# Two more chunks of an mLSTM + FFN kernel attended in 64x64 quarters, and two FFN stages exchanged

## The chip, the cores and the metric

The kernel runs on one core of a Trainium2 chip. The core has a tensor engine (PE in the profile; its weight loads are listed as PEld), a vector engine (DVE), a scalar engine (ACT), GpSimd (POOL) and a sync engine (SP), whose only work here is to issue DMA transfers (its queue is SPq in the profile). Each engine carries out its own instructions in the order in which the program puts them. The metric is the device time of one execution in microseconds (us). All values are 32-bit floats.

## What is computed

An mLSTM cell feeds a feed-forward network with a squared ReLU:

```python
# mLSTM cell: q, k, v, o_gate of shape (4, 8, 768, 40); i_gate, f_gate of shape (4, 8, 768)
for t in range(S):
    m_new = max(f[t] + m, i[t])
    f_stab, i_stab = exp(f[t] + m - m_new), exp(i[t] - m_new)
    m = m_new
    C = f_stab * C + i_stab * outer(v[t], k[t])       # 40 x 40 for each of 4 x 8 heads
    n = f_stab * n + i_stab * k[t]
    y[t] = sigmoid(o[t]) * (C @ q[t]) / max(abs(n @ q[t]), 1)
# FFN on x = y as (3072, 320)
h = maximum(x @ w_in, 0)                              # w_in 320 x 2048
out = (h * h) @ w_out                                 # w_out 2048 x 320
```

## The kernel before

**Chunks.** The 768 steps of each batch are cut into 6 chunks of 128 steps, so there are 24 chunks, numbered `s` = 0 to 23. Within a chunk the cell is an attention: scores of keys and queries, multiplied by a matrix of decays `W`, times the values; across chunks it hands on the state `C`. Two chunks make one group of 256 tokens for the FFN; FFN1 is the product with `w_in`, FFN2 the one with `w_out`. Groups 0 and 1 take FFN1 in full; groups from 2 on take it by a recursive scheme of fewer block products (`ffn1_open`, `ffn1_rows`, `ffn1_close`), and FFN2 of groups from 1 on likewise (`ffn2_fast`).

**Old and new way of attending.** Chunks 0 to 5 (`X_SQ = 6`) go through `attend`: matmuls `hi` (queries times old state, L622), `dC` (state update, L634) and `hp` (weighted scores times values, L645), then `normalise`, which leaves rows of `x` in SBUF; `turn_rows` transposes these rows on the tensor engine (L848, L850) and ACT copies them to `xT` (L853). Chunks from 6 on go through `attend_begin` and `attend_end`: the same products in quarters of 64x64, which the array works on side by side (L708 for the state, L727 for the values, L738 for the update). Between begin and end stands a one-element DVE instruction (L700), on which the second half of the matmuls waits. Their result is transposed: `store_num` writes it to DRAM (L773), `load_num` reads it back in four transfers (L778), `normalise_turned` divides it and multiplies with the gate on DVE (L787 to L803), `store_rows` and `load_rows` send `x` through DRAM once more (L828, four of L833), and `turn_squares` ends the transposition on DVE (L840). `scale_q` (L672) multiplies the queries by their decays on DVE; the products of L708 read its result. `decays` (L488) makes those decays on ACT.

**Masks.** `mask` (L469) sets the entries of late keys in `A` to -1e30 on POOL, and then `weigh` takes exponentials on ACT (L511), eight instructions for a chunk.

**Order of the work.** The order is written out by hand and kept on every engine. After a prologue, a loop over `u` = 0 to 7 takes chunks 2 to 5, two values of `u` a chunk, with a quarter of FFN1 of group 0 (`u` < 4) or 1 in each (L874, L885). In an odd `u` it calls `attend`, transfers for later chunks (`load`, `pair_up`, `load_o`) and `transposes` of the next chunk (L549); in an even one `scores` (L583), `weighted` (L597) and `weigh`. All along it rounds the weights to a shorter format, one piece after another: `words` on ACT (L220, L222), `join` on DVE (L231, L235, L236) and POOL (L240), and the fetch of a later piece (L210), which waits for the buffer that `join` has freed. The sums of weights for the recursive scheme (`sums_of_win`: L1020, L1022, L1024, L1026) stand on DVE between these. A second loop over `n` takes the rest in parts, four to a chunk, from chunk 6 on: FFN1 of group 2 with chunk 6, FFN2 of group 0 with chunk 7 (L911), and then FFN2 of group g with an even and FFN1 of group g + 2 with an odd chunk.

In the odd passes `u` = 5 and 7 the transfers that SP is given after `attend` are, in this order:

```python
for r in {5: (8,), 7: (9,)}.get(u, ()):
    load(r)                      # 7 transfers
for r in {5: (7,), 7: (8,)}.get(u, ()):
    pair_up(r)                   # 4 transfers
if u > 4:
    load_o(2 * s)
    load_o(2 * s + 1)
```

## Time and profile before

| | us |
|---|---|
| median of three runs (lowest, highest) | 491.84 (490.12, 493.88) |
| the profiled execution: its time | 491.22 |
| its span from first to last instruction | 489.4 |

Where each engine is busy in the stages that the change touches (busy us in each stretch of the span):

| stretch, us | what PE does | PE | DVE | ACT | POOL |
|---|---|---|---|---|---|
| 40 to 60 | FFN1 of group 0, chunk 3 | 18.51 | 16.70 | 15.69 | 9.97 |
| 60 to 76 | chunk 4, FFN1 of group 1 | 15.44 | 10.25 | 13.79 | 4.58 |
| 76 to 91 | chunk 5, FFN1 of group 1 | 15.00 | 12.56 | 12.16 | 6.38 |
| 91 to 110 | chunk 6, FFN1 of group 2 | 19.00 | 15.46 | 12.62 | 6.78 |
| 110 to 131 | chunk 7, FFN2 of group 0 | 20.72 | 18.39 | 11.28 | 10.01 |
| 131 to 167 | chunks 8 and 9 | 36.00 | 24.22 | 13.55 | 23.78 |

The granted clock of the tensor engine is 1.00 in each of these stretches. A row of a timeline reads: start in us from the beginning of the span, duration in us, engine, line of the kernel, operation, result<-operands, how many were merged ("x8"), and in brackets the idle time before it with what ended that. A row of the chain of waits has the same first two columns and names the work that the end of the program hangs on at that time. Rows for one kind of instruction can be told apart by their line. One f32 matmul counts as two PE instructions.

### The profile page before, as it was taken

To read this page: it belongs to the slowest core of one execution; us is meant where nothing else is said; L and a number is where in the kernel's file an instruction comes from. 1 tells how busy PE (TensorE), PEld (TensorE's weight loads), DVE (VectorE), ACT (ScalarE), POOL (GpSimd) and SP (SyncE) were. 2 spreads that over 40 slices of the span, in tenths; PEclk is the share of its full clock that TensorE was granted. 3 is DMA by queue.
4 is the path that set the end of the run, shared out by engine and by line. 5 is a ranking of instruction groups with operands and counts; after the bars stand their busy time and mean duration, and the time that the engine had idled before them with its cause. 6 is when DMAs were issued, how large, how long until landed. Compare 5 with 4: busy or idle time off the path is not lost.

```text
span 489.4 us, 15237 instructions
## 1 busy us (share of the span) xinstructions
PE 481.7 (98%) x6169; PEld 449.0 (92%) x6169; DVE 341.8 (70%) x704; ACT 240.4 (49%) x531; POOL 215.3 (44%) x322
## 2 busy tenths in 40 slices
PE   9999999999999999999999999999999999999997
PEld 4886788897799999999999999999999999999996
DVE  7799767888946856957966956857856956635441
ACT  4676996764522650942742941742942640513300
POOL 6455533432679178078179078078174040020000
PEclk9999999999999999999999999999999999999999
DMA  9999997745878579758759778658665612200000
GB/s 185 227 243 227 304 230 183 151 84 140 171 130 199 120 138 225 134 107 212 135 99 219 140 117 208 134 109 213 123 106 129 149 51 82 55 28 2 3 27 29
DMA packets 191096, 68.08 MB, mean 139 GB/s; under 512 B 158833, under 2 KB 180241, under 8 KB 191025
## 3 DMA queue, kind: packets, MB, share of 16 engines
q1 hardware_dynamic: 185280, 57.50, 55.1%
q0 software_dynamic: 5600, 9.50, 8.1%
q8 instruction: 49, 0.80, 0.7%
q14 instruction: 23, 0.18, 0.1%
q10 hardware_dynamic: 144, 0.10, 0.1%
HBM read 54.77 MB, written 18.01 MB: 149 GB/s over the span
## 4 chain that ended last, share of the span: by engine, by line
PE 87%; ACT 5%; SPq 4%; DMA 3%; issue 1%; DVE 0%; ACTq 0%
PE h_ps L965 35%; PE h_ps L1041 26%; PE h_ps L1090 8%; PE h_ps L911 4%; PE h_ps L874 3%; PE numT L727 3%; PE numT L708 2%; DMA lent_t<-in_moe_w_in_dram 1%; PE numT L738 1%; SPq L210 1%; PE tp L575 1%; PE h_ps L575 1%; SPq L1151 1%; ACT g_c L511 1%; DMA raw<-in_moe_w_in_dram 1%; DMA og<-in_o_gate_dram 1%
## 5 line engine op out<-in xcount | busy, mean ns | idle before, releaser
L475 POOL TENSOR_SCALAR_AFFINE_SELECT A_bc<-A_bc 64x512 f32<-64x512 f32 x32 | 22.5, 704 | 80.4 <-ACT kq L492 57.9
L965 PE MATMUL h_ps<-T,S 128*128 128x160 f32 x352 | 51.7, 300 | 0.6 <-ACT g_c L1107 0.6
L1071 ACT COPY r_sb<-h_ps 128x512 f32<-128x512 f32 x18 | 10.5, 585 | 84.2 <-PE h_ps L1041 84.2
L965 PEld LDWEIGHTS h_ps<-T,S 128*128 128x128 f32 x352 | 48.9, 190 | 1.1 <-ACT g_c L1107 0.9
L965 PE MATMUL h_ps<-w_out,g 128*128 128x160 f32 x336 | 49.2, 303 | 0.0
L981 DVE TENSOR_TENSOR y_sb<-y_sb,h_ps 128x160 f32<-128x160 f32 x44 | 14.1, 320 | 47.7 <-PE h_ps L965 47.6
L965 PEld LDWEIGHTS h_ps<-w_out,g 128*128 128x128 f32 x336 | 46.1, 190 | 1.3 <-issue 0.5
L1041 PE MATMUL h_ps<-xT,w_in 128*128 128x128 f32 x320 | 42.8, 278 | 0.0
L1041 PE MATMUL h_ps<-lent_t,w_in 128*128 128x128 f32 x320 | 42.2, 275 | 0.0
L1041 PEld LDWEIGHTS h_ps<-xT,w_in 128*128 128x128 f32 x320 | 38.9, 192 | 1.4 <-issue 1.0
L1090 PE MATMUL h_ps<-xT,w_in 64*64 64x128 f32 x960 | 39.1, 272 | 0.0
L1041 PEld LDWEIGHTS h_ps<-lent_t,w_in 128*128 128x128 f32 x320 | 38.9, 192 | 0.2 <-issue 0.2
L1041 PE MATMUL h_ps<-lent_t 128*128 128x128 f32 x320 | 39.0, 275 | 0.0
L1041 PEld LDWEIGHTS h_ps<-lent_t 128*128 128x128 f32 x320 | 37.3, 192 | 0.0
L505 ACT ACTIVATE A_bc<-A_bc,b_R 128x64 f32<-128x64 f32 (+1 forms) x128 | 35.7, 361 | 1.8 <-POOL A_bc L475 1.4
L1090 PEld LDWEIGHTS h_ps<-xT,w_in 64*64 64x64 f32 x960 | 34.8, 133 | 1.3
L379 POOL DMA_DIRECT2D va<-in_v_dram x56 | 34.2, 619 | 1.8 <-DMA kq_rows<-in_q_dram 1.3
L758 DVE STREAM_TRANSPOSE tn<-numT 128x256 f32<-128x256 f32 x36 | 14.0, 428 | 28.5 <-PE numT L708 19.2
L874 PE MATMUL h_ps<-xT,w_in 128*128 128x256 f32 x128 | 30.1, 385 | 1.6 <-ACT xT L853 1.2
L874 PEld LDWEIGHTS h_ps<-xT,w_in 128*128 128x128 f32 x128 | 23.4, 190 | 6.1 <-POOL w_in L240 1.6
L1033 POOL TENSOR_TENSOR lent_t<-xT 128x128 f32<-128x128 f32 (+1 forms) x18 | 14.6, 833 | 32.7 <-DVE xT L840 32.7
L965 PE MATMUL h_ps<-w_out,g_c 128*128 128x160 f32 x192 | 28.0, 302 | 0.0
(218 smaller groups left out, 1150.0 us busy)
## 6 DMA issues: line engine op xcount, KB each, us to landing
A_bc<-a_slots SPq DMA_DIRECT2D x32, 256.0 KB, 4.4
num_rows<-tn SPq DMA_DIRECT2D x18, 256.0 KB, 2.3
kq<-num_rows SPq DMA_DIRECT2D x72, 64.0 KB, 2.1
raw<-in_moe_w_out_dram SPq DMA_DIRECT2D x7, 640.0 KB, 5.4
kqT<-kq_rows SPq DMA_DIRECT2D x34, 128.0 KB, 3.3
og<-in_o_gate_dram SPq DMA_DIRECT2D x24, 160.0 KB, 4.9
out_dram<-y_sb SPq DMA_DIRECT2D x24, 160.0 KB, 3.1
raw<-in_moe_w_in_dram SPq DMA_DIRECT2D x7, 512.0 KB, 6.9
```

The source lines that it names most:

```text
L379: eng.dma_start(dst[HALVES[n], PR * (1 - late_keys) : PR * (2 - late_keys)], src[HALVES[late_keys], PR * m : PR * (m + 1)],)
L475: nc.gpsimd.affine_select(part, part, compare_op=ALU.is_ge, fill=-1e30, base=0, pattern=[[0, PR], [0, 2], [1, DP]], channel_multiplier=-1,)
L505: nc.scalar.activation(A[0][:, x, to], A[0][:, x, to], AF.Exp, bias=b_R[:, b, c, own, x : x + 1],)
L727: nc.tensor.matmul(d["numT"][m][HALVES[e], i, t0:], lhsT=va_w[s % NKQ][keys, at * D1 : at * D1 + DP], rhs=rhs, start=(s % NB == 0 and i == ...
L758: nc.vector.transpose(to[:, 2 * m : 2 * m + 2], d["numT"][m].rearrange("p c t -> p (c t)"))
L874: nc.tensor.matmul(hs[i][:, n, :], lhsT=w_in[:, a, fb * P : (fb + 1) * P], rhs=xT[:, :, a, :], start=(n == 0 and a == 0), stop=False,)
L911: nc.tensor.matmul(o_ps, lhsT=st["g2", g][:, fb, j * P : (j + 1) * P], rhs=w_out[:, fb, :], start=(fb == 0), stop=(fb == NF - 1),)
L965: nc.tensor.matmul(to, lhsT=lhsT[:, p], rhs=rhs[:, p, :], start=(start and p == 0), stop=(p == NPAIR - 1), skip_group_check=True,)
L981: add = lambda to, a, b: nc.vector.tensor_tensor(to, a, b, op=ALU.add)
L1033: sub = lambda to, a, b: eng.tensor_tensor(to, a, b, op=ALU.subtract)
L1041: nc.tensor.matmul(to[:, n, :], lhsT=lhsT[:, 4 * q + n, :], rhs=rhs, start=(start and n == 0), stop=True, skip_group_check=True,)
L1090: nc.tensor.matmul(to[cols, n, :], lhsT=w_in2[rows, 4 * q + n, cols], rhs=rhs, start=(start and n == 0), stop=True, skip_group_check=True,)
```

## The change

- `X_SQ` goes from 6 to 4: chunks 4 and 5 are attended by `attend_begin` and `attend_end`, stored by `store_num`, read back by `load_num`, normalised by `normalise_turned`, and their `x` goes through DRAM (`store_rows`, `load_rows`, `turn_squares`) and not through `turn_rows`. The state of chunk 3 is read in its old layout, that of chunk 4 is kept in the new one in the same buffers (`C_flat`).
- The masks of chunks 4 and 5 are no longer put on `A` ahead of the exponentials, but on `W` behind them (`mask_W`, one POOL instruction). `weigh(4)` and the new `decays(4)` move on ACT ahead of the rounding step that they followed.
- In the loop over `n`, FFN2 of group 0 comes first, with chunk 6, and FFN1 of group 2 second, with chunk 7. `ffn1_begin` goes; FFN2 of group 0 holds two PSUM banks at a time. The sums for the recursive scheme move with them.
- A constant mask (`bdm`) goes; one product with it becomes two copies.

The core of the diff:

```diff
-    KQ_SQ, X_SQ, ROT = 7, 6, 8
+    KQ_SQ, X_SQ, ROT = 7, 4, 8
...
+    def mask_W(s):
+        nc.gpsimd.affine_select(
+            st[s]["W"], st[s]["W"], compare_op=ALU.is_ge, fill=0.0, base=0, pattern=[[0, H], [1, P]],
+            channel_multiplier=-1,
+        )
...
     for u in range(8):
...
-                turn_rows(s - 1)
+                if s - 1 < X_SQ:
+                    turn_rows(s - 1)
                 scores(s)
                 ffn1(u // 4, u % 4)
             if u == 2:
+                weigh(4, masked=True, vw=False)
+                decays(4)
                 rounding.words()
             weighted(s)
...
             if u == 2:
-                mask(s + 1)
                 rounding.join()
+                mask_W(4)
                 rounding.join()
-                weigh(s + 1, masked=True)
+                values(4)
                 rounding.words()
             else:
...
-                weigh(s + 1, masked=(u == 0), vw=(u > 0))
+                if u == 6:
+                    normalise_turned(4)
+                    store_rows(4)
+                weigh(s + 1, masked=(u != 6), vw=(u == 6))
+                if u == 4:
+                    mask_W(5)
                 square_half()
+                if u > 0:
+                    scale_q(s)
...
-            attend(s)
+            if s < X_SQ:
+                attend(s)
+            else:
+                attend_begin(s)
+                attend_end(s)
...
-            normalise(s)
+            if s < X_SQ:
+                normalise(s)
+            else:
+                store_num(s)
...
             if u > 4:
                 load_o(2 * s)
                 load_o(2 * s + 1)
+            if u == 7:
+                load_rows(4)
+                load_squares(7)
+            if u > 4:
+                load_num(s)
             transposes(s + 1, (True, True))
             rounding.words()
             ffn1(u // 4, u % 4)
             square_half()
+            if u == 5:
+                decays(5)
...
-    turn_rows(5)
-    load_squares(7)
+    turn_squares(4)
...
-    parts = [(1, 2, i) for i in range(4)] + [(2, 0, i) for i in range(4)]
-    for g in range(1, NG):
+    parts = []
+    for g in range(NG):
         parts += [(2, g, i) for i in range(4)]
         if g + 2 < NG:
             parts += [(1, g + 2, i) for i in range(4)]
...
+        if n == 0:
+            turn_kq(7)
+            normalise_turned(5)
+            store_rows(5)
+        if n == 1:
+            load_rows(5)
```

On each engine the new order is the program's own. On DVE it is, from chunk 4 on: `weighted(4)`, `scale_q(4)`, a `join`, L700 of chunk 4, its two transposes, its state, a `join`, a sum of weights, `weighted(5)`, `normalise_turned(4)`, `scale_q(5)`, a `join`, a sum of weights, L700 of chunk 5, its transposes, two `join`s, a sum of weights, `turn_squares(4)`, `weighted(6)`, `turn_kq(7)`, `normalise_turned(5)`, a `join`, L700 of chunk 6. On SP `store_num(4)` comes right behind the fetch of the `join` that follows chunk 4's state, then `load(8)`, `pair_up(7)`, two `load_o`, and `load_num(4)` behind these; one chunk later a fetch and `store_num(5)`, `load(9)`, `pair_up(8)`, two `load_o`, `load_rows(4)`, `load_squares(7)` and `load_num(5)`.

## The prediction, made before the changed kernel ran

> **What bounds the kernel now.** I read the page's busy times first, then the chain of waits from 56 to 142 us, then the timelines of PE, ACT, DVE and SP over that stretch. The busy line says that the tensor engine has no room:
>
> ```profile
> PE 481.7 (98%) x6169; PEld 449.0 (92%) x6169; DVE 341.8 (70%) x704; ACT 240.4 (49%) x531; POOL 215.3 (44%) x322
> ```
>
> The chain tells where that holds. From 49 to 60.5 us it runs over ACT; from 60.56 us to the end it is PE with hardly a gap. So behind 60.56 us an instruction taken from PE is worth its whole length, and anything that PE has to wait for costs its whole length. The rows for the parts that change, the old attend of chunk 4, the transposition of its x, and the new attend (of chunk 7, from its first matmul to its last):
>
> ```profile
> 65.35 1.05 PE hi L622 x8
> 66.40 0.89 PE dC L634 x8
> 67.29 1.75 PE hp L645 x16
> ...
> 74.47 0.37 PE tp L848 x2
> 74.83 0.37 PE tp L850 x4
> ...
> 114.54 0.38 PE numT L708 x8
> ...
> 115.64 0.17 DVE kq L700
> ...
> 116.75 0.22 PE numT L708 x8
> ```
>
> Two idle times stand in the stretch before, in the timelines of ACT and PE: ACT waits 4.27 us for a piece of the weights, and PE then waits 1.16 us for ACT.
>
> ```profile
> 48.93 0.68 ACT L220 ACTIVATE mag<-raw 128x512 f32<-128x512 f32 x1 [4.27 <-DMA raw<-in_moe_w_in_dram]
> ...
> 60.56 0.70 PE L874 MATMUL h_ps<-xT,w_in 128*128 128x256 f32 x2 [1.16 <-ACT xT L853]
> ```
>
> The last view is the one that decides. It is SP's timeline behind chunk 4, with no gap in it from 70.04 to 78.80 us:
>
> ```profile
> 70.04 0.37 SPq L210 DMA_DIRECT2D raw<-in_moe_w_out_dram  x1
> 70.51 0.42 SPq L367 DMA_DIRECT2D kq<-in_k_dram  x1
> 71.02 1.28 SPq L369 DMA_DIRECT2D kq<-in_k_dram  x2
> 72.40 2.57 SPq L379 DMA_DIRECT2D va<-in_v_dram  x4
> 75.02 1.25 SPq L347 DMA_DIRECT2D kq_rows<-in_k_dram  x2
> 76.31 1.23 SPq L347 DMA_DIRECT2D kq_rows<-in_q_dram  x2
> 77.59 1.21 SPq L417 DMA_DIRECT2D og<-in_o_gate_dram  x2
> ```
>
> That is 0.64 us for each of 13 transfers. In the kernel before nobody is waiting for them.
>
> **What the change takes off PE.** The attend of chunk 4 goes from 3.70 us (65.35 to 69.05) to the 2.43 us of chunk 7 (114.54 to 116.97, its wait for L700 included): -1.27. That of chunk 5, the last of its batch, has no update; it goes from 2.80 (81.01 to 83.81) to two passes each of L708 and L727, 0.38 + 0.44 + 0.22 + 0.46 = 1.50: -1.30. The two `turn_rows` go, 0.73 (74.47 to 75.20) and 0.74: -1.47. Chunk 7's scores come as in later chunks, 0.69 for 0.88: -0.19. FFN1 of group 2 and FFN2 of group 0 keep their matmuls, so that exchange is worth nothing by itself.
>
> **What it moves on ACT.** `weigh(4)` (2.43 + 0.20 us, now at 50.08) and two new decays (0.61 each, chunk 6's row) are 3.85 us; they go into the idle 4.27, so ACT is some 2.6 us earlier behind it. PE gets its 1.16 back and 0.24 by which an FFN1 quarter was stretched (3.86 for 3.62): -1.4, with 0 as the other end, should the next piece of weights then be late (it is issued at 45.28 and lands a median of 5.4 us later, at 50.7, so I take the -1.4). The POOL masks are of like size in another place, 1.28 and 1.09 us, and the decays of chunk 5 (1.22) meet 1.55 us of ACT idle at 74.49: no cost; without that cover they would delay a ReLU by 1.2. The constant mask and one product against two copies are under 0.5 us on POOL and DVE in the prologue, where the chain runs over DMA and ACT: taken as 0.
>
> All this makes -5.6 us, if no wait is added.
>
> **The first added wait: chunk 5's scaled queries.** Chunk 4's result now has to be back from DRAM before DVE gets to `scale_q(5)`, because `normalise_turned(4)` stands in front of it in DVE's order. Count from PE. Chunk 4 starts at 65.35 - 1.4 and ends 2.43 later, at 66.4. DVE then transposes (0.78), updates the state (0.35) and does a `join` (1.88, from 68.10 to 69.98): 69.4. Only then can SP's fetch start, which the `join` releases. SP needs the 8.76 us of the rows above, and 0.34 and a gap for `store_num`: 78.6. Four reads of `load_num` take 1.73 us to issue and the last lands 2.1 later (its median): 82.1. `normalise_turned` is 1.84 (107.70 to 109.54), `scale_q` 0.65: 84.6. PE comes to chunk 5 at 66.4 + 0.90 (L549) + 4.53 (FFN1 quarter) + 1.09 (scores) + 4.71 (next quarter) = 77.6. It waits +7.0 us.
>
> **The second: L700 of chunk 5.** PE does its first half in 0.82, to 85.4. DVE has a `join` and a sum of weights (1.88 + 1.21) between `scale_q(5)` and L700 (0.17), so it is there at 88.0 at best: +2.6. Chunk 5 ends at 88.7.
>
> **The third: weights of chunk 6.** PE goes on for 0.90 + 4.52 + 1.09 + 4.50 (a quarter of FFN2), to 99.7. DVE has `turn_squares(4)` ahead of `weighted(6)`, and that waits for `load_rows(4)`. Chunk 5's transposes and a `join` end at 88.7 + 0.78 + 1.88 = 91.4; then SP has the fetch and 13 transfers, 9.66 us in its second series (84.45 to 94.11), and 0.45 for the store: 101.5. Four of L833 take 1.86 at the least and land 2.2 after the last: 105.1. DVE turns (0.53) and weighs the first half (0.64): 106.3. PE waits +6.6, and 0.2 more for the second half.
>
> **The fourth: L700 of chunk 6.** In front of it DVE has `turn_kq(7)`, `normalise_turned(5)` and a `join`. `load_squares(7)` takes 3.1 us to issue (mean of four rows) and lands 3.4 after its last: 109.1; `load_num(5)` lands at 109.9 by then. So 109.1 + 1.23 + 1.84 + 1.88 + 0.17 = 114.2. PE, at 107.2 with its first half and 0.69 of scores in between, waits +6.3.
>
> Chunk 6 then ends at 114.9, with scores, chunk and a quarter of FFN2 done; the same work ended at 91.06 + 4.50 + 1.48 + 0.88 = 97.9 before. Items: -5.6 + 7.0 + 2.6 + 6.8 + 6.3 = +17.1.
>
> Next in line are the sums over x for FFN1 of group 2. DVE has them about 126.3 (`load_num(6)` landed 121.9, then 1.84, 1.45 and 1.06), PE asks at 114.9 + 13.12 = 128.0: covered, by under 2 us, and that much could be lost too. From chunk 8 on the order on PE is the old one, and PE is the bound again.
>
> Against the profiled execution, 491.22 (0.6 under the median of the three runs, which is nothing here): 491.2 + 17.0 = 508.2. PE also starts slowly after idling. The kernel's first matmuls, in the timeline, run at 424 ns each (12 in 5.09 us), later ones of the same form at 220:
>
> ```profile
> 0.94 5.30 PE L1140 MATMUL idle<-zeros 128*128 128x512 bf16 x12 [0.94 <-DVE zeros L1135]
> 7.27 1.03 PE L1140 MATMUL idle<-zeros 128*128 128x512 bf16 x4
> ```
>
> No gap in this trace is longer than 1.2 us, and none of those shows it, so I bound it: nothing, or 12 x 0.204 = 2.45 us for each of three gaps over 6 us, 7.4 in all. Only the last gap is followed by work that PE bounds, so I take half of one, +1: 509.
>
> By the Trainium skill ("TensorE: Matmul & The Clock Gate", Part 1) the array falls to half its clock after an idle window of about 3.4 us and needs as long a busy one to recover. An estimate by that page is 1.7 us lost for each gap, 5.1 for three, which would make the sum 513; it speaks against a change that opens such gaps, and the trace before has none long enough to test it.
>
> **The rivals.** (a) Forecast: all four waits, chance 0.65. SP's spacing is its bound: at the 0.43 us that a lone `load_num` read takes in the trace, each 13 transfers would be 2.7 us shorter, 5.4 off: 503; all of the slow clock: 516. (b) Only the first two: the 7 us in which PE stands still let SP catch up, and the third and fourth are covered: 491.2 - 5.6 + 9.6 = 495. It needs a fetch, 14 transfers and three more sets of four between 91.4 and about 99 us, 0.3 us each; the rows say 0.64. Chance 0.12. (c) On the other side, faster: the reads of chunk 4 are there in time, PE stays without gaps, and the -5.6 are all: 485.6. It decides at 75.1 us, when the data must have landed for DVE to have `scale_q(5)` done at 77.6; that is 7 us earlier than my count. For it speaks that in later chunks store and read back take under 6 us (store at 101.67, reads issued from 103.71 to 106.02); against it, that there nothing is queued between them. Chance 0.08. (d) Worse than the forecast, from slow clock and transfers that land later than their medians together (x rows take up to 6.2 us): 516 and more. Chance 0.15.
>
> **How the numbers follow.** The time is that of (a), 509. The range takes in (a) with its bounds (503 to 516), nearly all of (b) and the lower part of (d): 494 to 517. One per cent, about what a measurement can tell, is 4.9 us: faster than 486.9 is (c), 0.08; within is most of (b), 0.11; slower is the rest, 0.81.
>
> **What would show it.** PE's idle time in front of chunk 5's first L708, put down to DVE, of about 7 us; behind it one of 2 to 3 us in front of the second half; DVE idle at the normalisation's first instruction (L790 now) for `num_rows`, and at L840 for `x_rows`; SP without a gap for 8 us between the store and its reads. The 1.16 us in front of the first quarter of group 1 should be gone, and each attend shorter by 1.3. If SP issues these 13 transfers in 2 us, or the reads stand ahead of them, I am wrong, and (c) holds.

## The result and the profile after

| | before | after |
|---|---|---|
| median, us (lowest, highest, runs) | 491.36 (490.12, 493.88, 4) | 523.37 (522.60, 524.29, 4) |
| ratio, 95% interval | | 1.0645 (1.0597 to 1.0694) |
| profiled execution: its time, its span | 491.22, 489.4 | 524.09, 522.4 |

The change makes the kernel 32 us slower. The forecast was slower too, but 509 us with a range to 517, so it is 14 us short and outside its range. In the tables, times are medians of all runs; the ratios leave out one run each of e2 and e15, which fell in a slower state of the chip. First the page of the changed kernel: the busy times, the granted clock in 40 slices, and the chain that ended last by engine.

```profile
PE 487.0 (93%) x6229; PEld 452.7 (87%) x6229; DVE 341.5 (65%) x719; ACT 242.5 (46%) x534; POOL 218.4 (42%) x321
...
PEclk9999996868889999999999999999999999999999
...
PE 76%; SPq 8%; DMA 7%; DVE 4%; ACT 3%; issue 2%; POOL 0%; DVEq 0%; ACTq 0%; POOLq 0%
```

PE stands still for 35.4 us of the span (522.4 - 487.0) where it was 7.7 before. It is also busy 5.3 us longer, although the quarters are meant to take less of its time; the clock row dips in slices 7 to 12 (78 to 157 us). The chain now runs 15% over SP's queue and transfers (7% before). PE's timeline, its rows behind an idle time of over 1 us from 78 to 165 us:

```profile
88.12 0.70 PE L727 MATMUL numT<-kq,Co 40*64 40x128 f32 x8 [8.53 <-DVE kq L687]
91.23 0.70 PE L727 MATMUL numT<-kq,Co 40*64 40x128 f32 x8 [1.55 <-DVE Co L718]
...
110.17 1.30 PE L746 MATMUL numT<-A_bc,va 64*64 64x128 f32 x16 [4.91 <-DVE A_bc L601]
113.52 2.08 PE L579 MATMUL h_ps<-kqT 40*64 40x128 f32 x32 [1.67 <-DVE kqT L405]
119.10 0.67 PE L757 MATMUL numT<-vw,kq 64*64 64x41 f32 x16 [3.50 <-DVE kq L718]
140.56 3.75 PE L1063 MATMUL h_ps<-lent_t 128*128 128x128 f32 x16 [4.98 <-DVE lent_t L1058]
```

L727, L746, L718, L687 and L601 of the changed kernel are L708, L727, L700, L672 and L597 of the kernel before. The first two rows are the first and second wait of the forecast, the third is its third, the next two together its fourth (it was split, since chunk 7's scores, L579, stand in the middle). The last was not forecast as a wait. The chain of waits of the changed kernel shows the first one piece by piece; it answers to SP's timeline before:

```profile
71.85 0.45 SPq L795
...
72.40 5.39 DMA kq<-in_k_dram
...
77.81 1.24 SPq L343
...
81.67 0.72 SPq L800
...
83.39 2.03 DMA kq<-num_rows
...
85.54 0.18 DVE dm L812
...
87.38 0.68 DVE kq L687
```

Chunk 4's result is stored at 71.85, and its first read (L800) is issued at 81.67: 13 transfers for later chunks lie between. They take 9.17 us (8.29 in the kernel before): in the chain the eighth of them (L343, 77.81) comes behind the landing of the first, 5.39 us after its issue. The last read lands 2.03 us after its issue; then come 1.84 us of normalising and `scale_q` (L687), on which PE waits.

The fifth wait, in ACT's timeline and then in DVE's:

```profile
130.41 0.42 ACT L939 COPY y_sb<-h_ps 128x320 f32<-128x320 f32 x1 [26.16 <-PE h_ps L933]
130.86 2.44 ACT L515 ACTIVATE A_bc<-A_bc,b_T 128x128 f32<-128x128 f32 x8
```

```profile
134.22 1.29 DVE L601 TENSOR_TENSOR A_bc<-h_ps,A_bc 128x512 f32<-128x512 f32 x2 [7.10 <-POOL vw L536]
```

ACT has nothing to do for 26.16 us, because the copy of FFN2's first result (L939) stands in its order ahead of chunk 7's exponentials (L515), and PE comes to that result only at 130.4. The exponentials feed `vw` on POOL, `vw` the weighting of chunk 7 on DVE, and behind the weighting, in DVE's order, stand `normalise_turned(6)` and the sums over x, for which PE waits 4.98 us. So two things make this wait together, as e4, e6 and e16 show: the copy ahead of the exponentials, and the weighting of chunk 7 ahead of `normalise_turned(6)`, which the change brought when it moved chunk 7's scores forward.

To tell where later runs gain, one length is useful: from the first matmul of FFN1 of group 1 behind chunk 3 (60.56 us before, 61.23 after) to the first of FFN2 of group 1 (130.84 and 161.50). It is 70.28 us before and 100.27 after. What lies ahead of it differs by up to 3 us between executions of kernels that have the same instructions there (59.23 us in e13, 62.20 in e10). What lies behind is 358.56 us before and 360.90 after; it differs too, 358.55 in e3 with the instructions of the changed kernel, and 361.29 in e8 with those of the kernel before.

### The profile page after: what moved, and what is told of

Its sections match the earlier page's. It is cut to its first block, busy times and chain, and to the rows that moved or that the text cites. A ratio compares the mean times of both kernels' runs of the same rounds, so it can differ in the third digit from the quotient of the medians.

```text
span 522.4 us, 15398 instructions
## 1 busy us (share of the span) xinstructions
PE 487.0 (93%) x6229; PEld 452.7 (87%) x6229; DVE 341.5 (65%) x719; ACT 242.5 (46%) x534; POOL 218.4 (42%) x321
## 4 chain that ended last, share of the span: by engine, by line
PE 76%; SPq 8%; DMA 7%; DVE 4%; ACT 3%; issue 2%; POOL 0%; DVEq 0%; ACTq 0%; POOLq 0%
PE h_ps L987 33%; PE h_ps L1063 25%; PE h_ps L1096 7%; PE numT L746 3%; DMA lent_t<-in_moe_w_in_dram 3%; PE numT L727 2%; PE h_ps L933 2%; PE numT L757 1%; DMA raw<-in_moe_w_in_dram 1%; SPq L206 1%; DMA raw<-in_moe_w_out_dram 1%; SPq L413 1%; SPq L1156 1%; PE h_ps L579 1%; DMA kq<-in_k_dram 1%
## 5 line engine op out<-in xcount | busy, mean ns | idle before, releaser
L478 POOL TENSOR_SCALAR_AFFINE_SELECT A_bc<-A_bc 64x512 f32<-64x512 f32 x32 | 24.4, 763 | 86.5 <-ACT kq L496 69.5
L1077 ACT COPY r_sb<-h_ps 128x512 f32<-128x512 f32 x20 | 11.7, 585 | 86.3 <-PE h_ps L1063 86.3
L1063 PE MATMUL h_ps<-lent_t 128*128 128x128 f32 x320 | 40.8, 283 | 5.0 <-DVE lent_t L1058 5.0
L1063 PEld LDWEIGHTS h_ps<-lent_t 128*128 128x128 f32 x320 | 39.0, 199 | 5.1 <-issue 5.1
L236 POOL TENSOR_TENSOR w_out<-mag,low 128x640 int32<-128x640 int32 x7 | 13.4, 1914 | 40.5 <-DVE mag L232 37.7
```

The lines of the kernel that those rows point to most:

```text
L236: nc.gpsimd.tensor_tensor(dst.bitcast(I32), bits, low.bitcast(I32), op=ALU.add)
L478: nc.gpsimd.affine_select(part, part, compare_op=ALU.is_ge, fill=-1e30, base=0, pattern=[[0, PR], [0, 2], [1, DP]], channel_multiplier=-1,)
L1063: nc.tensor.matmul(to[:, n, :], lhsT=lhsT[:, 4 * q + n, :], rhs=rhs, start=(start and n == 0), stop=True, skip_group_check=True,)
```

## The experiments

| run | change against | us | ratio to before, 95% interval | length, us |
|---|---|---|---|---|
| e1 | after: first reads early | 521.79 | 1.0602 (1.0578 to 1.0627) | 98.38 |
| e2 | after: normalising later | 516.73 | 1.0490 (1.0457 to 1.0523) | 93.11 |
| e3 | after: PE kept busy | 520.54 | 1.0588 (1.0542 to 1.0635) | 98.37 |
| e4 | after: exponentials first | 517.08 | 1.0514 (1.0477 to 1.0552) | 94.27 |
| e5 | after: second exchange first | 517.78 | 1.0514 (1.0497 to 1.0530) | 94.70 |
| e6 | before: FFN stages exchanged | 492.51 | 1.0003 (0.9989 to 1.0017) | 70.67 |
| e7 | after: all reordered | 505.26 | 1.0285 (1.0244 to 1.0326) | 83.32 |
| e8 | before: early exponentials | 491.33 | 0.9975 (0.9963 to 0.9988) | 70.28 |
| e9 | e7: SP unblocked | 503.34 | 1.0248 (1.0201 to 1.0294) | 78.88 |
| e10 | e9: chunk 7's scores late | 504.32 | 1.0267 (1.0238 to 1.0296) | 79.76 |
| e11 | e10: rows turned last | 505.64 | 1.0267 (1.0231 to 1.0304) | 82.05 |
| e12 | e11: loads last | 506.85 | 1.0288 (1.0251 to 1.0326) | 76.42 |
| e13 | after: no exchanges | 510.81 | 1.0396 (1.0315 to 1.0478) | 87.02 |
| e14 | e4: no exchanges | 504.65 | 1.0227 (1.0179 to 1.0276) | 81.52 |
| e15 | e14: scores late | 493.36 | 1.0007 (0.9985 to 1.0030) | 70.33 |
| e16 | after: scores late | 519.30 | 1.0537 (1.0508 to 1.0566) | 96.33 |
| e17 | e15: normalising later | 492.39 | 1.0017 (0.9995 to 1.0039) | 68.93 |
| e18 | e4: scores late | 518.65 | 1.0529 (1.0486 to 1.0572) | 95.36 |

Each ratio is to runs of the kernel before on the same chip (medians from 491.1 to 493.4 us), so times of runs on different chips can differ by some 2 us without any cause in the kernel. My theory at the start was the forecast's: the time is lost in waits for the exchanges over DRAM, and the order on SP makes them. The rivals: the slower clock behind each gap, ACT's order, the exchange of the FFN stages.

**e1: chunk 4's reads right behind its store.**

```diff
+            if u == 5:
+                load_num(s)          # ahead of load(8), pair_up(7), load_o
...
-            if u > 4:
+            if u == 7:
                 load_num(s)
```

> Edit: in pass u = 5 alone, load_num(4) stands directly behind store_num(4), ahead of load(8), pair_up(7) and the two load_o. Theory Q (the order on SP and DVE makes the waits): the reads are issued some 2 us after the store at 71.9, land about 78, DVE has scale_q(5) at about 80.5, so PE's first wait falls from 8.5 us to 1 or so; the chain of waits behind chunk 5 stays as it is but starts 8 us earlier. Time 512 to 516 (changed kernel: 523.4). Theory X (the exchange of FFN2 and FFN1, or the early exponentials, cost the time): no change, 522 to 525.

Measured 521.79 us, hardly less than the changed kernel and far from theory Q's figure. SP's timeline:

```profile
71.93 0.45 SPq L795 DMA_DIRECT2D num_rows<-num  x1
76.93 2.61 SPq L800 DMA_DIRECT2D kq<-num_rows  x4
```

SP stands still for 4.55 us until the store has landed, where the same pair in the kernel before is 2.04 us apart (101.67, 103.71). The first wait falls from 8.53 to 4.20, but SP's later transfers move back: a new wait of 1.52 us comes in front of FFN2, and the third grows from 4.91 to 6.18.

**e2: chunk 4 normalised later on DVE.** `normalise_turned(4)` and `store_rows(4)` go from `u` = 6 behind `store_num(5)` in `u` = 7, so that `scale_q(5)` has no wait in front of it.

```diff
-                if u == 6:
-                    normalise_turned(4)
-                    store_rows(4)
...
+            if u == 7:               # behind attend_end(5), store_num(5)
+                normalise_turned(4)
+                store_rows(4)
```

> Edit: normalise_turned(4) and store_rows(4) stand behind store_num(5) in pass u = 7, no longer ahead of scale_q(5); SP's order is as in the changed kernel but for store_rows(4). Theory Q: the first wait of 8.5 us and the second of 1.6 go, chunk 5 ends 11 us earlier, near 81.5; but x of chunk 4 then goes out at about 87.5 with load(9) and the rest behind it on SP, so weighted(6) is ready near 102 where PE asks at 92.5: the third wait grows from 4.9 to about 10 us. Time 513 to 517. If the wait were DVE's own length and not the data's way through DRAM, the third wait would not grow and the time would be near 510. Theory X: 522 to 525.

Measured 516.73. The first and the second wait, 10.1 us together, shrink to 0.28, but a gap of 2.85 us opens in front of FFN2 and the third wait grows to 6.30: of 10 us, 6.6 are gained, as theory Q had it.

**e3: PE kept busy.** Dummy matmuls (34, 22, 8, 12 and 20 of 128x512) are put where PE waits; they change no result.

```diff
+                if u == 7:
+                    idle(34)
                 attend_begin(s)
...
+            if n == 1:               # 8 and 12 more around chunk 7's scores
+                idle(22)
             do(attend_begin, s)
...
+        if g == 2 and q == 0:        # in ffn1_open
+            idle(20)
```

> Edit: dummy matmuls of 128x512 bf16 (some 0.22 us each) are put into the five places where PE waits: 34 ahead of chunk 5, 22 ahead of chunk 6, 8 ahead of chunk 7's scores, 12 behind them, 20 behind the first block of group 2's FFN1; each bunch is shorter than the wait that it stands in. Nothing else moves. Theory C (the slow clock after a gap is what the prediction mis-sized): the mean granted clock goes from 0.967 to over 0.99, the matmuls behind the gaps run at their old durations (eight transposes in 1.1 us and not 1.97), and of the 9 us that PE's work took longer behind gaps, 5 to 8 come off the end: 515 to 519. If the slow clock only fell into time that other engines set: 521 to 524.

Measured 520.54, between the two figures and 2.8 us less than the changed kernel; the intervals of the two ratios overlap, so even this gain is only a best estimate. The windows of the changed kernel and of e3 (columns: stretch, length, busy us of PE, PEld, DVE, ACT and POOL, granted clock, DMA share, GB/s):

```profile
78.50:88.10 9.60, 1.10 (x9) 0.65 (x8) 2.42 (x11) 3.61 (x7) 0.74 (x1) 0.66 0.43 96
...
110.20:120.60 10.40, 5.24 (x97) 4.07 (x97) 5.42 (x15) 0.00 (x0) 1.59 (x2) 0.50 0.31 64
```

```profile
78.50:88.10 9.60, 8.46 (x60) 3.93 (x58) 3.27 (x12) 2.33 (x5) 0.00 (x0) 1.00 0.47 104
...
110.20:120.60 10.40, 8.85 (x120) 5.05 (x121) 6.86 (x21) 0.00 (x0) 2.05 (x2) 1.00 0.40 72
```

The clock is 1.00 instead of 0.66 and 0.50, but PE goes on behind the gaps at nearly the same moments (87.25, 90.36, 110.60, 114.48, 118.64 and 138.44, against 88.12, 91.23, 110.17, 113.52, 119.10 and 140.56). So what DVE waits for, and not PE, sets these moments; with faster matmuls PE merely has longer to wait.

**e4: chunk 7's exponentials ahead of FFN2's copy on ACT.**

```diff
         elif g == 0:
+            if at == 2:
+                do(lambda s: weigh(s, masked=True), s + 1)
             ffn2(g, i % 2, i // 2)
...
         if at == 2:
-            do(lambda s: weigh(s, masked=True), s + 1)
+            if n > 3:
+                do(lambda s: weigh(s, masked=True), s + 1)
```

> Edit: in part n = 2 alone, weigh(7) is called ahead of ffn2, so that on ACT the eight exponentials no longer stand behind the copy of FFN2's result. Theory Q in its second form (an order on ACT, brought by the exchange, makes the fifth wait): DVE's idle 7.1 us ahead of weighted(7) goes, the sums over x are ready before PE asks, the fifth wait of 5.0 us goes and the first blocks of group 2's FFN1 run at full clock (2.7 us): 515 to 518.5. If the data of chunk 6 through DRAM set that place as the prediction had it: 521 to 524.

Measured 517.08: the fifth wait is gone and 6.3 us with it, as expected.

**e5: the second exchange ahead of the prefetches.** `load_rows(4)`, `load_squares(7)` and `load_num(5)` go ahead of `load(9)`, `pair_up(8)` and `load_o`.

```diff
+            if u == 7:
+                load_rows(4)
+                load_squares(7)
+                load_num(s)
             for r in {5: (8,), 7: (9,)}.get(u, ()):
                 load(r)
...
-            if u == 7:
-                load_rows(4)
-                load_squares(7)
-            if u > 4:
+            if u == 5:
                 load_num(s)
```

> The changed kernel, with the second exchange with DRAM (load_rows(4), load_squares(7), load_num(5)) issued ahead of load(9), pair_up(8) and load_o; the first exchange is left as it is. Theory (the second exchange is late because some 8 us of SP issues stand ahead of its reads): the third wait (4.91 us before the second half of the row-wise attend of chunk 6) goes, the fourth (1.67 + 3.50) falls to about 3, the fifth (4.98) stays; 513 to 515 us. Rival (the exchange waits for the store of turn_squares on its way to DRAM, not for SP's order, as the first exchange did when its reads were put forward): the third and fourth waits keep 8 us or more between them, 520 to 525 us.

Measured 517.78, between the two. The third wait is gone as the theory said, but the fourth keeps 0.40 + 4.44 and the first grows to 9.92.

**e6: the two FFN stages exchanged, alone.** The kernel before, with FFN2 of group 0 ahead of FFN1 of group 2; chunks 4 and 5 keep the old way, and chunk 7's scores stay behind FFN2 (`n` = 4). The sums, rounding steps and transfers of this stretch move with the stages, as in the change.

```diff
-    parts = [(1, 2, i) for i in range(4)] + [(2, 0, i) for i in range(4)]
-    for g in range(1, NG):
+    parts = []
+    for g in range(NG):              # FFN2 of g, then FFN1 of g + 2
...
```

> The kernel before with one part of the change: FFN2 of the first group stands ahead of FFN1 of the third group; chunks 4 and 5 are attended row-wise as before, with their masks as before. Theory A (my prediction: the exchange is worth nothing by itself): 490 to 494 us. Theory B (the copy of FFN2's y on ScalarE now stands ahead of the exponentials of chunk 7 and so makes the fifth wait by itself): a wait of 4 to 5 us before the first matmul of the gate sums or of FFN1 of the third group, 496 to 499 us.

Measured 492.51, no wait: theory A. ACT's copy stands ahead of the exponentials here too, but nothing that PE needs soon is queued behind chunk 7's weighting.

**e7: all of the change, reordered by hand**, with e4 in it and the reads ahead of a part of the prefetches.

```diff
+            if u == 5:               # behind load(8)
+                load_num(s)
...
+            if u == 7:               # behind attend_end(5)
+                store_num(s)
+                normalise_turned(4)
+                load_squares(7)
+                store_rows(4)
+                load_num(s)
...
-    turn_squares(4)
...
+            turn_squares(4)          # n == 0, behind weighted(6)
...
+        if n == 1:                   # behind attend_end(6)
+            normalise_turned(5)
+            store_rows(5)
```

> The changed kernel with all of its work, in another order: the exponentials of chunk 7 ahead of FFN2's copy; the reads of both exchanges ahead of the prefetches of weights and inputs; normalise_turned(4) behind chunk 5's transposes and normalise_turned(5) behind the end of chunk 6's attend; turn_squares(4) behind weighted(6). Theory (the quarters save the PE time that was forecast, and every added microsecond is a wait that the order makes): the five waits fall to 5 us or less in sum, 486 to 495 us. Rival (the quarters cost VectorE, ScalarE and the DMA queues so much in this stretch that the waits come back elsewhere): 500 to 515 us.

Measured 505.26: the rival's figure. Two waits of over 2 us are left, 3.31 us before FFN2 and 6.04 in chunk 6.

**e8: the early exponentials, alone**, in the kernel before (without the new `decays(4)`).

```diff
             if u == 2:
+                weigh(4, masked=True, vw=False)
                 rounding.words()
...
-                mask(s + 1)
                 rounding.join()
+                mask_W(4)
                 rounding.join()
-                weigh(s + 1, masked=True)
+                values(4)
...
```

> The kernel before with one part of the change: the exponentials and masks of chunks 4 and 5 are made on W ahead of time as in the change, their attends stay row-wise. Theory A (my prediction's term of -1.4: ScalarE's earlier exponentials let FFN1's quarter start sooner): the quarter starts at about 59.2 in place of 60.56, 490 to 491 us. Theory B (the quarter waits for a piece of weights that lands late, so nothing is won): it starts at 60.5 to 61.3, 491.5 to 493 us.

Measured 491.33, between the two figures; by the ratio 0.25% faster than the kernel before (0.12 to 0.37). ACT's timeline in e8:

```profile
48.97 0.68 ACT L220 ACTIVATE mag<-raw 128x512 f32<-128x512 f32 x1 [1.82 <-DMA raw<-in_moe_w_in_dram]
...
52.36 0.81 ACT L220 ACTIVATE mag<-raw 128x640 f32<-128x640 f32 x1 [2.14 <-DMA raw<-in_moe_w_out_dram]
```

The exponentials do move into the old idle time, and ACT then idles for the next piece of weights instead: the quarter starts at 60.43 (60.56 before) and the length stays at 70.28, so theory B holds for the mechanism. The changed kernel shows the same idle time for the second piece:

```profile
53.15 0.79 ACT L216 ACTIVATE mag<-raw 128x640 f32<-128x640 f32 x1 [2.37 <-DMA raw<-in_moe_w_out_dram]
```

Where the 1 us of e8's time comes from this profile can't show; its execution, 493.79, was the longest of twelve.

**e9 to e12: one wait after the other taken away.** e9 unblocks the weights' fetch and puts the exchange ahead of `load_squares(7)` and `load(9)` on SP.

```diff
                 normalise_turned(4)
-                load_squares(7)
                 store_rows(4)
                 load_num(s)
+                load_rows(4)
+                load_squares(7)
...
+        if u == 6:                   # behind the rounding steps
+            pair_up(7)
+            load_o(8)
+            load_o(9)
```

> The kernel of the run e7 with three moves on SP's queue alone: pair_up(7) and the two load_o of u=5 go behind the next fetch of weights (which they held back by 4.4 us in e7, to 84.26); store_rows(4), load_num(5) and load_rows(4) go ahead of load_squares(7) (which stood 6.35 us in front of them, waiting for pair_up); load_rows(4) goes ahead of load(9). Theory (what is left of the added time in e7 is the waits of 3.31 us before FFN2 and 6.04 us in chunk 6's attend, and both come from the order on SP): both fall under 1 us, 490 to 496 us; if the quarters then save the forecast 4.2 us of TensorE, it comes to 488 to 491. Rival (the exchanges themselves load SP, VectorE and the DMA queues, so that another wait takes their place): 499 to 506 us.

Measured 503.34, inside the rival's figure: the two waits are down to 2.38 and 1.21 us, and one of 2.79 comes in front of chunk 7's scores. e10 moves chunk 7's scores back (the diff stands with e15) and the normalising behind the rounding:

```diff
-                normalise_turned(4)
             if u != 3:
                 rounding.join()
+            if u == 7:
+                normalise_turned(4)
```

> The kernel of the run e9 with two moves: the scores of chunk 7 and turn_kq(7) go back from n = 0 and 1 to n = 4 and 2, where the run e6 has them (in e9 turn_kq(7) waits 7.56 us for its rows and holds VectorE and the fetch of weights), and normalise_turned(4) goes behind the rounding's join in u=7 (in e9 it makes ScalarE's words wait 2.27 us for the last piece, and FFN2 2.38 us for g). Theory (what is left of the added time in e9 is again order: scores(7) moved forward by the change, and VectorE's row work ahead of the rounding): the waits of 2.38, 2.79 and 1.21 us go, the clock stays above 0.95 and the end is 8 to 10 us earlier, 492 to 496 us. Rival (PE is now 3.7 us ahead of the rounding of the weights and waits for it wherever FFN2 stands): FFN2 still waits 2 us or more and the time is 497 to 504 us.

Measured 504.32, above both figures: FFN2's wait falls from 2.38 to 0.45, and a new one of 6.26 us comes in chunk 6, for chunk 4's rows in front of L718. e11 puts `turn_squares(4)` behind the attend:

```diff
             do(attend_end, s)
+            if n == 1:
+                turn_squares(4)
```

> The kernel of the run e10 with two moves: turn_squares(4) goes behind the end of chunk 6's attend on VectorE (in e10 it waits 6.17 us for its rows with that attend's half way step queued behind it, and TensorE stands still for 6.26 us), and load_rows(4) goes ahead of load_num(5) on SP. Theory (what is left is one in-order wait, and its removal is paid in full): the 6.26 us go and the slower matmuls behind them, some 1.5 us more; 495 to 498 us. Rival (the exchange chain of chunk 5 and the sums over x of the third group need their time whatever stands first): the wait comes back before the lent_t matmuls of FFN1, 1.25 us in e10, as 4 us or more; 500 to 504 us. On either, 4 to 6 us over the kernel before are left, which are waits of the second exchange in FFN1 of the third group and not the work of the quarters.

Measured 505.64, above both figures, with the rival's mechanism: the wait has moved to the sums over x. PE's timeline, then DVE's:

```profile
121.95 3.79 PE L1063 MATMUL h_ps<-lent_t 128*128 128x128 f32 x16 [9.49 <-DVE lent_t L1058]
```

```profile
115.68 0.58 DVE L862 STREAM_TRANSPOSE xT<-xT 128x384 f32<-128x384 f32 x1 [11.50 <-DMA xT<-x_rows]
```

e12 moves the prefetches behind chunk 5's rows, and the last rounding step ahead of `turn_squares(4)`:

```diff
             do(load_num, s)
+            if n == 1:               # from u = 7
+                pair_up(8)
+                load(9)
+                load_o(10)
+                load_o(11)
             do(load_squares, s + 2)
```

> The kernel of the run e11 with load(9), pair_up(8) and two load_o moved on SP behind the last exchange of x (store_rows(5), load_rows(5)), and the last step of the rounding put ahead of turn_squares(4). In e11 the rows of chunk 5 are normalised at 100.1 us and stored at 107.7, since those 13 transfers stand between; the rows then come back at 115.7 and TensorE stands still for 9.49 us. Theory (the whole added time is waits for the exchange, each made by what stands ahead of it on an in-order queue): the stored rows leave at 100.5 and are back by 108, the 9.49 us fall under 2, the 1.95 us before FFN2 goes, and the time is 491 to 495 us, within 1% of the kernel before. Rival (the exchanges of chunks 4 and 5 in series are longer than the work that stands over them, whatever the order): TensorE still waits 4 us or more, 497 to 504 us.

Measured 506.85, outside both. PE's timeline:

```profile
114.70 3.79 PE L1063 MATMUL h_ps<-lent_t 128*128 128x128 f32 x16 [5.01 <-DVE lent_t L1058]
...
144.66 4.60 PE L987 MATMUL h_ps<-T,S 128*128 128x160 f32 x16 [5.11 <-DVE S L982]
```

Half of the 9.49 us is gone, and a wait of 5.11 us has come in chunk 7's exchange: DVE is held up there 7.56 us for rows whose reads are issued at 137.86, 5.2 us behind their store at 132.64. What makes that store slow is not shown. The five orders from e7 to e12 gave 503 to 507; in each a wait came back elsewhere. This made me doubt that the exchanges were all of it, and the next runs take them out.

**e13 and e14: no exchanges over DRAM for chunks 4 and 5.** The instructions on all compute engines stay; stores and reads go, and DVE reads the tiles in SBUF, so the rows of x of these two chunks are in the wrong order. These runs take away the waits for the exchanges and the traffic of their transfers at once, and can't tell the two apart. e13 is the changed kernel without them, e14 is e4 without them.

```diff
     def store_num(s):             # load_num, store_rows, load_rows alike
+        if s < NB:
+            return
...
-        nc.vector.transpose(t, t)
+        nc.vector.transpose(t, t if s >= NB else st[s]["x"][:])
...
```

> The changed kernel with the four exchanges over DRAM of chunks 4 and 5 left out (num and x, 2 stores and 8 reads of each chunk's pair): normalise_turned and the turn of x read the tiles in SBUF as they stand, with the same instructions on VectorE, so the rows of x for these two chunks are in the wrong order and the output differs from the reference. Everything else is the change's. Theory (the quarters save the forecast TensorE time, and all that was added is waiting for the exchanges): the first, second and third waits go, the fourth falls to 2 us or less; what is left is the fifth, some 5 us, which ScalarE's order makes: 489 to 495 us. Rival (the quarters themselves, the early masks or FFN2's place cost time apart from the exchanges): 500 us or more.

> The run e13 with the exponentials of chunk 7 ahead of FFN2 as in the run e4; the same exchanges of chunks 4 and 5 are left out. Theory (with e13's): no wait over 1 us is left before FFN1 of the third group, and the time falls below the kernel before by the forecast saving of TensorE and ScalarE, 4.2 to 5.6 us: 485 to 488 us. Rival (the fifth wait is not ScalarE's order but the late rows themselves): no more than 1 us below e13.

Measured 510.81, the rival's figure, and 504.65, outside both: ACT's order is worth 6.2 us here too, as the theory of e14 had it, but the time stays some 12 us above the kernel before on the same chip. With no exchange left, the tensor engine still waits in chunk 6. e14, PE's timeline and then DVE's:

```profile
102.16 2.08 PE L579 MATMUL h_ps<-kqT 40*64 40x128 f32 x32 [7.36 <-DVE dm L818]
...
105.95 0.67 PE L757 MATMUL numT<-vw,kq 64*64 64x41 f32 x16 [1.70 <-DVE kq L718]
```

```profile
100.86 1.25 DVE L405 STREAM_TRANSPOSE kqT<-kqT 128x1024 f32<-128x1024 f32 x1 [9.99 <-DMA kqT<-kq_rows]
```

These are chunk 7's scores. The change moves them, and `turn_kq(7)` with them, from behind FFN2 into chunk 6's attend; SP issues the reads of their rows (`load_squares(7)`) only at 94.75, behind all prefetches.

**e15 and e16: chunk 7's scores back.**

```diff
-        if at == 0 and even:
+        if at == 0 and (even or s == 7):
             do(scores, s)
...
-        if n == 0:
+        if n == 2:
             turn_kq(7)
```

> The run e14 (no exchanges over DRAM for chunks 4 and 5, so that their rows of x are in the wrong order; exponentials of chunk 7 first), with the scores of chunk 7 and turn_kq(7) back at n = 4 and 2, where the kernel before and the run e6 have them. Theory (the added time has two sources apart from ScalarE's order: the exchanges, and the scores of chunk 7, which the change puts into chunk 6's attend while their rows, kq_rows, are read late on SP): the waits of 7.36 us before scores(7) and 1.70 us behind it go with the slower matmuls after them, and the saving on TensorE shows: 487 to 492 us. Rival (something else of the quarters costs the rest): 498 us or more.

> The changed kernel, exchanges and all, with the scores of chunk 7 and turn_kq(7) back at n = 4 and 2. Theory (as for e15; but here chunk 6's attend also waits for the exchanges, which stand in front on SP and VectorE, so that the two sources lie side by side): the fourth wait (1.67 + 3.50 us) goes at most, the third (4.91) stays, 516 to 521 us. Rival (the two add up): 10 us or more come back, 508 to 513 us.

e15 takes 493.36 us, its ratio can't be told from 1: the theory's mechanism, just above its figure. The PE waits of e15 behind 56 us (us in total, times, longest), the first two of six:

```profile
PE numT L727 <- DVE Co L718: 1.8, 1, 1.8
PE h_ps L906 <- ACT xT L885: 1.2, 1, 1.2
```

Nothing long is left, so exchanges, scores and ACT's order together are all of the added time.

e16 takes 519.30, inside the theory's figure, but not by its mechanism. The third and fourth wait stay (5.08 and 7.02 us); it is the fifth that is gone. Chunk 7's weighting now stands behind `normalise_turned(6)` and the sums over x on DVE, which are done at 132.7, although the exponentials still start behind the copy, at 132.32.

**e17 and e18: the saving, and the exchanges by themselves.** e17 moves `normalise_turned(4)` in e15 behind the rounding's join (the same edit as in e2); e18 is e4 with the scores back, so it differs from e15 in the exchanges alone.

> The run e15 (no exchanges of chunks 4 and 5, so their rows of x are in the wrong order), with normalise_turned(4) moved from ahead of chunk 5's attend to behind the rounding's join after it. Theory (the forecast saving of 4.2 us on TensorE is there, and in e15 a wait of 1.82 us in chunk 5's attend, from VectorE's row work ahead of its half way step, and the slower matmuls behind it eat it): 488 to 490.5 us, ratio about 0.993 to 0.996. Rival (the saving does not reach the end even without a wait, because the weights' rounding sets the pace of this stretch): 492 us or more.

> The changed kernel, exchanges in place, with both other sources taken out: chunk 7's exponentials ahead of FFN2's copy (e4) and chunk 7's scores and turn_kq(7) back at n = 4 and 2 (e16). It differs from e15 in the exchanges alone. Theory (e4 gave 6.3 us and e16 4.1, and they add up): 511 to 515 us, so that the exchanges alone are worth 18 to 22 us. Rival (once both are gone the exchanges' waits close up, or another takes their place): under 508 or over 517 us.

e17 takes 492.39, ratio 1.0017 (0.9995 to 1.0039): the rival's figure. Its page says:

```profile
PE 477.8 (97%) x6229; PEld 445.1 (91%) x6229; DVE 339.8 (69%) x719; ACT 242.4 (49%) x534; POOL 218.9 (45%) x321
```

PE has 3.9 us less to do than before (481.7), but the length is only 1.35 us shorter. A wait of 1.94 us is still in it, in chunk 6, for DVE, which has no gap in its timeline from 81.15 to 95.22 us; three `join`s are 5.5 us of that. So the rival has something for it: in this stretch DVE's own work, the rounding with it, holds PE. What lies behind is 361.14 us, 2.6 more than before, with gaps of 1.28 and 0.70 us for which the profile names no cause; as e8 and e3 show, single executions differ by that much there with the same instructions. No run tried this further.

e18 takes 518.65, the rival's figure: the exchanges alone are worth 25.3 us (e18 less e15). Ordered by what is in them:

| us | scores early, copy first (as changed) | scores early, exponentials first | scores late, exponentials first |
|---|---|---|---|
| with exchanges | 523.37 (after) | 517.08 (e4) | 518.65 (e18) |
| without | 510.81 (e13) | 504.65 (e14) | 493.36 (e15) |

Down a column the exchanges cost 12.6, 12.4 and 25.3 us; along the lower row ACT's order costs 6.2 and the scores 11.3, along the upper row 6.3 and nothing (1.6 the other way). They do not add up, for two reasons. The edits of e4 and of e16 each take away the same fifth wait, so the second of them finds it gone (e18). And the wait for chunk 7's rows lies side by side with that for chunk 5's rows: the fourth wait ends at 120.01 us with the scores early (e4) and at 119.55 with them late (e18), so their early place costs something only when the exchanges are out.

## Why the prediction was wrong in its range, and right in its sign

Against the profiled executions the forecast was +18 and the result +32.9 us. By the forecast's terms:

| term | forecast, us | measured, us | from |
|---|---|---|---|
| quarters and no `turn_rows` | -4.2 | -3.9 | PE busy, e17 against before |
| earlier start of the quarter | -1.4 | +0.7 | 61.23 against 60.56 |
| first wait | +7.0 | +8.53 | PE's timeline |
| second wait | +2.6 | +1.55 | |
| third wait | +6.8 | +4.91 | |
| fourth wait | +6.3 | +5.17 | 1.67 + 3.50 |
| sums over x, "covered" | 0 | +4.98 | e4: 6.3 of the time |
| slower clock behind gaps | +1 | +9.2 | PE busy, 487.0 against 477.8 in e17 |
| behind FFN2 of group 1 | 0 | +2.3 | 360.90 against 358.56 |

The measured column sums to 33.4, against 33.0 us that the span grew. Its second row and its last are no larger than what executions with the same instructions differ by.

**Right:** that the prefetches between store and reads make the first wait, that the other three follow in order, and the four together (22.7 forecast, 20.2 measured). SP took 10.3 us from the fetch to the first read where I counted 9.2. PE's saving was sized right. The two FFN stages by themselves cost nothing (e6). Rivals (b) and (c) are out: the third and fourth wait came, and no read was in time. The time fell on the side of (d), for which I had 0.15, though not mainly by its late transfers.

**The step that failed:** "Next in line are the sums over x for FFN1 of group 2 [...]: covered, by under 2 us, and that much could be lost too". PE waited 4.98 us for them. I counted the chain from `load_num(6)` over DVE and did not look at what DVE had in front of it: chunk 7's weighting, whose exponentials the exchange of the FFN stages puts behind a copy of FFN2's result on ACT. Undoing that order gives 6.3 us (e4), and so, in part, does moving the weighting back (e16, 4.1). It is the rule that the prediction applied to SP and DVE, and not to ACT.

**Mis-sized:** the slower clock. I bounded it by 7.4 and took 1; the matmuls ran 9.2 us longer, at a granted clock between 0.50 and 0.93 in the six stretches from 78.5 to 161.5 us. By the Trainium skill ("TensorE: Matmul & The Clock Gate", Part 1) an idle window of some 3.4 us halves the clock, and it takes a busy one as long to bring it back; four gaps of the changed kernel reach that, an estimate by the page of 6.8 us. The windows agree in kind (0.50 at the least) and the size is near, but gaps of half that length slowed the clock too (last section). And e3 says that only some 2.8 us of the 9.2 reach the end: in a chain set by transfers a faster PE waits for longer. The third and fourth wait came out 3 us smaller than forecast; that this is the other side of it is likely, not shown.

**The -1.4 did not show.** I kept 0 as its other end, should the next piece of weights be late, and chose the -1.4. It was late: ACT idles 2.37 us for it in the changed kernel (53.15), and 2.14 in e8. The +0.7 by itself says little, since the quarter starts anywhere from 59.23 to 62.20 us in kernels with these instructions.

**Chunk 7's scores, forecast at -0.19.** While the exchanges stay, their early place costs little by itself (e18 is 1.6 us above e4). But it brought the weighting of chunk 7 ahead of `normalise_turned(6)`, and so one half of the fifth wait, which I did not see; its end in e16 (4.1 us) is that half. With the exchanges out it costs 11.3 us (e14 less e15), since the wait for their rows then has no cover.

**Open:** why e17, with 3.9 us less on PE, is not faster than before, and whether some other order could hide the exchanges; of the five that reorder all of it (e7, e9 to e12) none came under 503 us. No version with the quarters was faster than the kernel before.

## What to carry to other kernels

When work moves between two in-order engines, list for each engine what now stands ahead of the moved work and ahead of its readers, the quiet engines too: a copy on ACT, with 26 us of idle time in front of it, cost 6 us here. Waits that lie side by side cover each other, so undoing them one by one can understate them; and a wait that two orders make together goes with either, so two edits can gain it once only. Take the suspected cause out altogether to see what is left. Round trips over DRAM for which PE does not wait in one place (the chunks from 6 on in the kernel before) cost up to 25 us in another, where less work stands over them and prefetches fill the queue; which of the two counts for how much, no run here tells.

## What the runs showed of the hardware

- A store to DRAM and the first read of it on the same queue are 2.04 us apart in the kernel before, where SP had issued nothing for 4 us ahead of the store (101.67 to 103.71), and 5.00 us in e1, where a fetch of weights had been issued just ahead of it (71.93 to 76.93). The Trainium skill ("DMA: Bandwidth & Descriptors", "Anatomy of one DMA — SWDGE (gpsimd) path") puts the fixed cost at about 2 us, most of it the receipt of the write, for another issuing path; the quiet case agrees, the busy one is more than twice that.
- The clock granted in the six stretches of the changed kernel from 78.5 to 161.5 us was 0.66, 0.71, 0.93, 0.50, 0.93 and 0.87; with matmuls that fill the gaps (e3) it was 1.00 in five of them and 0.72 in the other, for some 2.8 us of time.
- A gap can slow the clock though it is much shorter than the 3.4 us of the page, and the same gap need not. Behind 1.82 us of idle time in e15 the granted clock fell to 0.50 (84 to 86 us); behind 1.81 us in e14 the same matmuls ran at full speed. The quarter of FFN1 behind that gap, in PE's timelines of e15 and of e14:

```profile
84.18 4.98 PE L906 MATMUL h_ps<-xT,w_in 128*128 128x256 f32 x16
```

```profile
83.30 3.62 PE L906 MATMUL h_ps<-xT,w_in 128*128 128x256 f32 x16
```
